# A running maximum spread over the partitions through DRAM instead of by 32-row products: an mLSTM cell and its SwiGLU block

## The chip, the cores and the metric

The kernel runs on one core of one Trainium2 chip. The core has TensorE (products, written PE in the profile, its weight loads PEld), VectorE (DVE), ScalarE (ACT), GpSimd (POOL) and SyncE (SP, which here only issues transfers), and 16 DMA engines that they share. The metric is the device time of one execution in microseconds; less is better. The median of the runs is used.

## The reference, cut to what matters

The first part is an mLSTM cell (batch 4, 8 heads, 768 tokens, heads of 40), given as a loop over tokens:

```python
for t in range(S):
    m_new = np.maximum(f_gate[:, :, t] + m, i_gate[:, :, t])
    f_stab = np.exp(f_gate[:, :, t] + m - m_new)
    i_stab = np.exp(i_gate[:, :, t] - m_new)
    m = m_new
    C = f_stab * C + i_stab * np.einsum('bhd,bhe->bhde', vt, kt)
    n = f_stab * n + i_stab * kt
    h_tilde = np.einsum('bhde,bhe->bhd', C, qt)
    denom = np.maximum(np.abs(np.einsum('bhd,bhd->bh', n, qt)[:, :, None]), 1.0)
    y[:, :, t] = sigmoid(o_gate[:, :, t]) * h_tilde / denom
```

The second part treats y as 3072 tokens of 320 features: out = (silu(x @ w_gate) * (x @ w_val)) @ w_out, with 1536 hidden features. The weights arrive as fp64, everything else as fp32, and all products are in fp32.

## The kernel before, in words

**Tiling.** The 768 tokens of a batch are cut into six chunks of 128 (the constant L). A chunk of a batch is a unit; batch b has units 6b to 6b + 5, 24 in all. Within a chunk the recurrence is written in closed form: F is the running sum of f, g = i - F, and M the running maximum of g and of what is carried in. Token s then acts on token t >= s with the weight w[s, t] = exp(g_s - M_t). The gates lie with a row per (batch, head), so on 32 partitions (f_sb, i_sb, F_sb, g_sb, M_sb, lines 68 to 139). The weights w need g with the token s on the partition (g_T, made by transposes) and M_t the same on all 128 partitions.

**Spreading M.** `weigh(b)` (line 222) makes w for the six chunks of a batch. For each head a product with 32 rows is used: one column of the negated identity `nid`, repeated 128 times, is the stationary operand, and M_sb of the chunk the moving one, so that each of the 128 output rows holds -M of that head (`nm`, line 230; 8 of them in a chunk, 192 in four batches of six chunks, which the profile counts as 384 matrix instructions since an fp32 product takes two here). VectorE adds g (line 232, twice in a chunk), GpSimd sets the part with t < s to -1e30 (line 234), ScalarE takes the exponential (line 236). The w tiles live in a pool of NB + 1 = 7 buffers.

**The cell of a unit** has five stages: `turn` loads the k, q, v and o of the unit two later, weighs v with w's last column (v_w, GpSimd) and transposes k and q; `scores` takes the k.q products (sp) and multiplies them with w on VectorE (s_sb, line 264); `attend` has the products with the state (inter), for the state (add) and with v (intra); `rows` normalises and applies the o gate's sigmoid; `seam` transposes the result into xT. k and q, v, and o have rings of three buffers.

**The block of a batch** has 30 steps: twice twelve `hidden` steps (gv_ps: six products with wg_sb, six with wv_sb; then a sigmoid on ScalarE, line 345, and two multiplications on VectorE, lines 346 and 347) and three `project` steps (o_ps, line 352). The first half of the steps reads the xT of chunks 0 to 2, the second that of 3 to 5. gv_ps and o_ps share two PSUM buffers.

**Order.** The program first weighs batch 0 and runs its cell, with the 24 pieces of the fp64 weights converted among the stages (`weight`, lines 195 to 209, on VectorE, ScalarE and GpSimd). Then, for each batch, the next batch is weighed and its cell's 30 stages run one after each of the block's 30 steps. This program order is a priority only: the Tile framework's planner writes the order of each engine's instructions by simulating the program, and issues on each engine the first in priority whose operands and buffers are ready at that point. At run time each engine then keeps that order and waits where something is late. SP's queue holds the loads of the cells and the stores of the output, ACT's queue those of the weights.

Of the kernel before, what the change touches and what calls it, by code (L numbers as in the profile page):

```python
# [9 lines left out]
F32 = mybir.dt.float32  # L10
U32 = mybir.dt.uint32
AF = mybir.ActivationFunctionType
ALU = mybir.AluOpType
AX = mybir.AxisListType
PSUM = bass.MemoryType.PSUM

L = 128  # tokens of a chunk
NEG = -1e30
# [3 lines left out]
def kernel(  # L22
# [12 lines left out]
):  # L35
    """mLSTM in chunks of 128 tokens, then the SwiGLU block, all in fp32.

    Within a chunk, F is the running sum of f, g = i - F and M the running maximum of g and of the m carried in, so
    that m = F + M. A token s adds exp(g_s - M_t) (k_s.q_t) [v_s, 1] to token t >= s, the state C of the chunks before
    adds exp(m_in - M_t) C q_t. No exponent is above 0 whatever the gates are. Weights that come as fp64 (as the bits  # L40
    of their words) are rounded to fp32 on the way in.
    """
    nc = tc.nc
    B, H, S, D = q.shape
    BH = B * H
    NB = S // L
    PR = H // 2  # pairs of heads, a head in each half of the partitions
    DP = 64
    D1 = D + 1
# [7 lines left out]
    const = ctx.enter_context(tc.tile_pool(name="const", bufs=1))  # L57
    wpool = ctx.enter_context(tc.tile_pool(name="wpool", bufs=1))
    dpool = ctx.enter_context(tc.tile_pool(name="dpool", bufs=NB + 1))
# [3 lines left out]
    psum = ctx.enter_context(tc.tile_pool(name="psum", bufs=2, space=PSUM))  # L63
    gates_scope = ExitStack()
    gates = gates_scope.enter_context(tc.tile_pool(name="gates", bufs=1))

# [1 line left out]
    f_sb = gates.tile([BH, NB, L], F32)  # L68
# [35 lines left out]

# [1 line left out]
    ident = const.tile([128, 128], F32)  # L106
    make_identity(nc, ident)
    idb = ident[0:BH, 0:BH]
    nid = const.tile([BH, BH], F32)
    nc.vector.tensor_scalar(nid, idb, scalar1=-1.0, scalar2=None, op0=ALU.mult)  # L110
    # which pair a row of the gates belongs to, and which half
    pair = const.tile([BH, B * PR], F32)
    nc.vector.reduce_sum(pair, idb.rearrange("p (a two) -> p a two", two=2), axis=AX.X)
    half = const.tile([BH, 2], F32)
    nc.vector.reduce_sum(half, idb.rearrange("p (a two) -> p two a", two=2), axis=AX.X)
    halves = const.tile([BH, 2, DP], F32)
    nc.vector.tensor_copy(halves, half.unsqueeze(2).to_broadcast([BH, 2, DP]))
    # a pair's state is kept whole; a head's own part of it is its half's columns
    own = const.tile([128, 2 * D1], F32)
# [8 lines left out]

# [1 line left out]
    def flat(t):  # L130
        return t.rearrange("p c t -> p (c t)")
# [5 lines left out]
    nc.vector.tensor_copy(step[:, 1:, 0:1], F_sb[:, 0:NB - 1, L - 1:L])  # L137
    M_sb = const.tile([BH, NB, L], F32)
    nc.vector.tensor_tensor_scan(flat(M_sb), flat(step), flat(g_sb), NEG, op0=ALU.add, op1=ALU.max)
    m_in = gates.tile([BH, NB - 1, 1], F32)  # L140
    nc.vector.tensor_add(m_in, M_sb[:, 0:NB - 1, L - 1:L], F_sb[:, 0:NB - 1, L - 1:L])
# [3 lines left out]

    # token on the partition: g_T[t, c, bh] and, for the chunks from the second, e_T
    g_T = const.tile([128, NB, BH], F32)
# [6 lines left out]

    # the decay of a whole chunk, spread over the partitions of the state
    dec_r = gates.tile([BH, NB - 1, B * PR], F32)
# [9 lines left out]

# [1 line left out]
    conv_scope = ExitStack()  # L168
# [4 lines left out]
    def weight(dst, src):  # L173
# [15 lines left out]
        else:  # L189
            nc.scalar.dma_start(out=raw, in_=src.bitcast(U32))  # L190
        words = raw.rearrange("p (n two) -> p n two", two=2)
        lo, hi = words[:, :, 0], words[:, :, 1]
        # The upper word's 20 bits of mantissa with 8 of its 11 bits of exponent; 0 for what fp32 has no exponent for.
        top = tmp("top", U32)
# [5 lines left out]
                                       op0=ALU.is_ge, op1=ALU.mult)  # L200
        # The lower word's bits, scaled by the sign and the power of two, round into it.
        power = tmp("power", U32)
# [15 lines left out]

# [1 line left out]
    w_tiles = {}  # L220

    def weigh(b):
        for c in range(NB):
            w = w_tiles[b * NB + c] = dpool.tile([128, 2, PR, L], F32, name="w_sb", tag="w")
            g2 = g_T[:, c, b * H:(b + 1) * H].rearrange("p (j two) -> p two j", two=2)
            for two in range(2):
                nm = psum.tile([128, PR, L], F32, name="nm", tag="att")
                for j in range(PR):
                    row = b * H + 2 * j + two
                    nc.tensor.matmul(nm[:, j, :], lhsT=nid[:, row:row + 1].to_broadcast([BH, 128]), rhs=M_sb[:, c, :],  # L230
                                     start=True, stop=True)
                nc.vector.tensor_tensor(w[:, two], nm, g2[:, two].unsqueeze(2).to_broadcast([128, PR, L]), op=ALU.add)  # L232
            wf = w.rearrange("p a j t -> p (a j) t")
            nc.gpsimd.affine_select(wf, wf, compare_op=ALU.is_ge, fill=NEG, base=0, pattern=[[0, H], [1, L]],  # L234
                                    channel_multiplier=-1)
            nc.scalar.activation(wf, wf, AF.Exp)

# [1 line left out]
    state = {}  # L239
    xts = {}  # L240

    def turn(u):
        un = units[u]
        load(u + NR - 1)
        un["v_w"] = work.tile([128, H, D1], F32, name="v_w")
        last = w_tiles[u][:, :, :, L - 1].rearrange("p two j -> p j two").unsqueeze(3).to_broadcast([128, PR, 2, D1])
        nc.gpsimd.tensor_tensor(un["v_w"].rearrange("p (j two) d -> p j two d", two=2),  # L247
                                un["v"].rearrange("p (j two) d -> p j two d", two=2), last, op=ALU.mult)
        for n, name in enumerate(("kT", "qT")):
            tp = psum.tile([128, PR, L], F32, name="tp_kq", tag="tr")  # L250
            for j in range(PR):
                nc.tensor.transpose(tp[:, j, :], un["kq"][:, n, 2 * j:2 * j + 2, :].rearrange("p h d -> p (h d)"), ident)  # L252
            un[name] = work.tile([128, PR, L], F32, name=name)
            nc.scalar.copy(un[name], tp)  # L254

    def scores(u):
        un = units[u]
        un["s"] = work.tile([128, 2, PR, L], F32, name="s_sb")
        for two in range(2):
            sp = psum.tile([128, PR, L], F32, name="sp", tag="att")  # L260
            r = slice(two * DP, two * DP + DP)
            for j in range(PR):
                nc.tensor.matmul(sp[:, j, :], lhsT=un["kT"][r, j, :], rhs=un["qT"][r, j, :], start=True, stop=True)  # L263
            nc.vector.tensor_tensor(un["s"][:, two], sp, w_tiles[u][:, two], op=ALU.mult)

# [64 lines left out]

# [1 line left out]
    hs = {}  # L332
# [31 lines left out]

# [1 line left out]
    weigh(0)  # L366
# [10 lines left out]
    for b in range(B):  # L377
        cell = []
# [41 lines left out]
```

## Time and profile before

| what | value |
|---|---|
| runs | 925.11, 924.93 and 929.82 us; median 925.11 |
| the profiled execution: time by its span, first to last instruction | 925.1 us |
| TensorE busy | 875.6 us (95%) |
| VectorE busy | 337.9 us (37%) |
| ScalarE busy | 156.1 us (17%) |
| GpSimd busy | 120.8 us (13%) |
| mean granted TensorE clock | 0.939 |
| moved by DMA | 32.22 MB, 35 GB/s on average |

How to read it: a row such as `L230 PE MATMUL nm<-M_sb,nid ... x384 | 79.9, 395 | 2.1 <-DVE w_sb L232` is a group of instructions: its line, engine, what it writes and reads, how many, their busy time in us and the mean in ns, and the idle time of the engine just before them with what ended it. The chain of waits goes back from the last instruction to what released each. In the chain by time and in timelines, a row starts with the start and the length in us. In rows of stretches come the length, then the busy time of PE, PEld, DVE, ACT and POOL, then the granted TensorE clock (1.00 is full speed), the DMA engines' share and GB/s. A row of DMA issues ends with the KB of one transfer and the median time from issue to landing.

### The profile page before, as it was taken

How to read it: one execution, taken by the hardware profiler on the slowest of the kernel's cores; microseconds unless marked ns; L12 is line 12 of the kernel's file. 1: busy time of each engine (PE TensorE's matmuls, PEld its weight loads, DVE VectorE, ACT ScalarE, POOL GpSimd, SP SyncE). 2: the span in 40 equal slices, each digit the busy share in tenths (PEclk: the TensorE clock that was granted, in tenths of full speed). 3: DMA queues.
4: the chain of work that ended last, by engine and by line, in shares of the span. 5: the costliest groups of instructions: out<-in, count | busy, mean ns of one | idle time of the engine just before them, and what ended most of it. 6: DMA issues, size and time to landing. Idle time of an engine off the chain costs nothing.

```text
span 925.1 us, 8778 instructions
## 1 busy us (share of the span) xinstructions
PE 875.6 (95%) x3477; PEld 553.0 (60%) x3477; DVE 337.9 (37%) x625; ACT 156.1 (17%) x274; POOL 120.8 (13%) x127
## 2 busy tenths in 40 slices
PE   6856769999999999999999999999999999999998
PEld 5755557855665568755665568655755565445445
DVE  5588877433214322334213322234313321210220
ACT  2322122311111112311111112311111101100110
POOL 2344434400000001100000002100000000000000
PEclk9999855599999999799999998799999999999999
DMA  9244454011021111011111110011100000000000
GB/s 139 64 108 112 116 132 114 1 21 30 15 44 21 29 18 33 7 25 27 27 31 22 29 29 22 7 29 22 37 14 1 1 8 14 1 0 22 0 1 21
DMA packets 107273, 32.22 MB, mean 35 GB/s; under 512 B 100640, under 2 KB 103712, under 8 KB 107232
## 3 DMA queue, kind: packets, MB, share of 16 engines
q1 hardware_dynamic: 103392, 19.87, 12.0%
q10 hardware_dynamic: 3840, 11.80, 4.1%
q8 instruction: 27, 0.44, 0.2%
q14 instruction: 14, 0.11, 0.0%
HBM read 27.72 MB, written 3.93 MB: 34 GB/s over the span
## 4 chain that ended last, share of the span: by engine, by line
PE 92%; DVE 3%; issue 1%; DMA 1%; POOL 1%; ACT 0%; ACTq 0%; DVEq 0%; POOLq 0%
PE gv_ps L341 49%; PE o_ps L352 17%; PE nm L230 8%; PE intra L293 5%; PE sp L263 5%; PE inter L273 3%; PE tp_kq L252 3%; PE add L280 2%; PE tp_x L319 1%; DVE top L196 1%; POOL wv_sb L209 0%; DVE size L204 0%; DMA raw<-in_moe_w_gate_dram 0%; DVE top L195 0%; DVE power L203 0%
## 5 line engine op out<-in xcount | busy, mean ns | idle before, releaser
L341 PE MATMUL gv_ps<-xT,wg_sb 128*128 128x384 f32 (+1 forms) x576 | 237.4, 531 | 0.0
L341 PE MATMUL gv_ps<-xT,wv_sb 128*128 128x384 f32 (+1 forms) x576 | 233.5, 526 | 0.0
L341 PEld LDWEIGHTS gv_ps<-xT,wv_sb 128*128 128x128 f32 (+1 forms) x576 | 94.4, 190 | 130.2 <-issue 103.6
L352 PE MATMUL o_ps<-wo_sb,h_sb 128*128 128x320 f32 x576 | 159.3, 435 | 0.0
L341 PEld LDWEIGHTS gv_ps<-xT,wg_sb 128*128 128x128 f32 (+1 forms) x576 | 96.1, 194 | 99.8 <-issue 76.5
L352 PEld LDWEIGHTS o_ps<-wo_sb,h_sb 128*128 128x128 f32 x576 | 108.1, 190 | 44.7 <-issue 1.1
L346 DVE TENSOR_TENSOR sg<-sg,gv_ps 128x384 f32<-128x384 f32 x96 | 53.1, 553 | 221.7 <-ACT sg L345 221.7
L345 ACT ACTIVATE sg<-gv_ps 128x384 f32<-128x384 f32 x96 | 47.1, 490 | 335.7 <-PE gv_ps L341 335.6
L347 DVE TENSOR_TENSOR h_sb<-sg,gv_ps 128x384 f32<-128x384 f32 x96 | 53.2, 554 | 118.8 <-PE gv_ps L341 118.8
L230 PE MATMUL nm<-M_sb,nid 32*128 32x128 f32 x384 | 79.9, 395 | 2.1 <-DVE w_sb L232 1.1
L230 PEld LDWEIGHTS nm<-M_sb,nid 32*128 32x128 f32 x384 | 76.0, 300 | 5.8 <-DVE w_sb L232 3.6
L247 POOL TENSOR_TENSOR v_w<-va,w_sb 128x328 f32<-128x328 f32 x24 | 18.1, 752 | 315.0 <-PE add L280 254.3
L293 PEld LDWEIGHTS intra<-va,s_sb 128*128 128x128 f32 x384 | 54.2, 221 | 3.5 <-issue 0.3
L293 PE MATMUL intra<-va,s_sb 128*128 128x41 f32 x384 | 53.8, 306 | 0.0
L263 PEld LDWEIGHTS sp<-qT,kT 64*128 64x128 f32 x384 | 47.1, 228 | 10.8 <-ACT qT L254 4.8
L263 PE MATMUL sp<-qT,kT 64*128 64x128 f32 x384 | 48.6, 324 | 3.2 <-ACT qT L254 3.2
L232 DVE TENSOR_TENSOR w_sb<-nm,g_T 128x512 f32<-128x512 f32 x48 | 33.2, 691 | 39.6 <-PE nm L230 39.4
L310 POOL TENSOR_TENSOR x_sb<-o_sb,y_sb 128x320 f32<-128x320 f32 x24 | 20.8, 869 | 190.3 <-DVE y_sb L296 187.2
L252 PE MATMUL tp_kq<-ident,kq 128*128 128x128 f32 x192 | 34.1, 323 | 7.3 <-DVE xT L324 5.2
L319 PE MATMUL tp_x<-ident,x_sb 128*128 128x128 f32 (+1 forms) x72 | 14.9, 323 | 25.5 <-DVE x_sb L311 25.5
L252 PEld LDWEIGHTS tp_kq<-ident,kq 128*128 128x128 f32 x192 | 25.5, 164 | 20.6 <-issue 9.9
L234 POOL TENSOR_SCALAR_AFFINE_SELECT w_sb<-w_sb 128x1024 f32<-128x1024 f32 x24 | 26.6, 1108 | 82.5 <-DVE w_sb L232 82.5
(70 smaller groups left out, 494.3 us busy)
## 6 DMA issues: line engine op xcount, KB each, us to landing
kq<-in_k_dram SPq DMA_DIRECT2D x24, 160.0 KB, 3.0
kq<-in_q_dram SPq DMA_DIRECT2D x24, 160.0 KB, 2.8
va<-in_v_dram SPq DMA_DIRECT2D x24, 160.0 KB, 2.6
o_sb<-in_o_gate_dram SPq DMA_DIRECT2D x24, 160.0 KB, 2.6
raw<-in_moe_w_out_dram ACTq DMA_DIRECT2D x6, 640.0 KB, 4.0
out_dram<-z_sb SPq DMA_DIRECT2D x24, 160.0 KB, 1.8
raw<-in_moe_w_gate_dram ACTq DMA_DIRECT2D x6, 512.0 KB, 3.7
raw<-in_moe_w_val_dram ACTq DMA_DIRECT2D x6, 512.0 KB, 3.6
```

The lines of the kernel that those rows point to most:

```text
L230: nc.tensor.matmul(nm[:, j, :], lhsT=nid[:, row:row + 1].to_broadcast([BH, 128]), rhs=M_sb[:, c, :], start=True, stop=True)
L232: nc.vector.tensor_tensor(w[:, two], nm, g2[:, two].unsqueeze(2).to_broadcast([128, PR, L]), op=ALU.add)
L234: nc.gpsimd.affine_select(wf, wf, compare_op=ALU.is_ge, fill=NEG, base=0, pattern=[[0, H], [1, L]], channel_multiplier=-1)
L252: nc.tensor.transpose(tp[:, j, :], un["kq"][:, n, 2 * j:2 * j + 2, :].rearrange("p h d -> p (h d)"), ident)
L263: nc.tensor.matmul(sp[:, j, :], lhsT=un["kT"][r, j, :], rhs=un["qT"][r, j, :], start=True, stop=True)
L273: nc.tensor.matmul(inter[:, 2 * j:2 * j + 2, :].rearrange("p h d -> p (h d)"), lhsT=un["qT"][:, j, :], rhs=state["C"][:, j, :], start=True ...
L293: nc.tensor.matmul(intra[:, h, :], lhsT=un["s"][:, h % 2, h // 2, :], rhs=un["v"][:, h, :], start=True, stop=True)
L341: nc.tensor.matmul(p, lhsT=w_sb[0:dn, kc, ts(m, 128)], rhs=xts[b][0:dn, kc, ts(n, TW)], start=(kc == 0), stop=(kc == NKC - 1))
L345: nc.scalar.activation(sg, ps[0], AF.Sigmoid)
L346: nc.vector.tensor_tensor(sg, sg, ps[0], op=ALU.mult)
L347: nc.vector.tensor_tensor(hs[b, n][:, m, :], sg, ps[1], op=ALU.mult)
L352: nc.tensor.matmul(p, lhsT=hs[b, n][:, m, ts(i, 128)], rhs=wo_sb[:, m, :], start=(m == 0), stop=(m == NFC - 1))
```

## The change

M no longer passes through TensorE. After the scan that makes it, M_sb (32 rows of 768) is stored into a scratch tensor in DRAM, M_dram. For each chunk one transfer then reads the eight heads' 128 values and writes them to all 128 partitions, straight into the w tile: the source has a step of 0 over the partitions, so that each partition receives eight runs of 512 bytes. VectorE computes g - M in one subtraction over 1024 elements from SBUF to SBUF, where it had two additions over 512 elements from PSUM; GpSimd's select and ScalarE's exponential stay as they are. The heads in the w tile now stand in their own order instead of even ones first, and `scores` and `turn` read it by other strides. M_sb moves to the pool of the gates, whose memory the weights' conversion uses later; `nid` is gone.

```diff
-    nid = const.tile([BH, BH], F32)
-    nc.vector.tensor_scalar(nid, idb, scalar1=-1.0, scalar2=None, op0=ALU.mult)
...
-    M_sb = const.tile([BH, NB, L], F32)
+    M_sb = gates.tile([BH, NB, L], F32)
     nc.vector.tensor_tensor_scan(flat(M_sb), flat(step), flat(g_sb), NEG, op0=ALU.add, op1=ALU.max)
+    M_dram = tc.dram_tile([BH, S], F32, name="M_dram")
+    nc.sync.dma_start(out=M_dram, in_=flat(M_sb))
...
         for c in range(NB):
-            w = w_tiles[b * NB + c] = dpool.tile([128, 2, PR, L], F32, name="w_sb", tag="w")
-            g2 = g_T[:, c, b * H:(b + 1) * H].rearrange("p (j two) -> p two j", two=2)
-            for two in range(2):
-                nm = psum.tile([128, PR, L], F32, name="nm", tag="att")
-                for j in range(PR):
-                    row = b * H + 2 * j + two
-                    nc.tensor.matmul(nm[:, j, :], lhsT=nid[:, row:row + 1].to_broadcast([BH, 128]), rhs=M_sb[:, c, :],
-                                     start=True, stop=True)
-                nc.vector.tensor_tensor(w[:, two], nm, g2[:, two].unsqueeze(2).to_broadcast([128, PR, L]), op=ALU.add)
-            wf = w.rearrange("p a j t -> p (a j) t")
-            nc.gpsimd.affine_select(wf, wf, compare_op=ALU.is_ge, fill=NEG, base=0, pattern=[[0, H], [1, L]],
+            w = w_tiles[b * NB + c] = dpool.tile([128, H, L], F32, name="w_sb", tag="w")
+            src = M_dram[b * H:(b + 1) * H, ts(c, L)].unsqueeze(0).to_broadcast([128, H, L])
+            nc.sync.dma_start(out=w, in_=src)
+            gb = g_T[:, c, b * H:(b + 1) * H].unsqueeze(2).to_broadcast([128, H, L])
+            nc.vector.tensor_tensor(w, gb, w, op=ALU.subtract)
+            nc.gpsimd.affine_select(w, w, compare_op=ALU.is_ge, fill=NEG, base=0, pattern=[[0, H], [1, L]],
                                     channel_multiplier=-1)
-            nc.scalar.activation(wf, wf, AF.Exp)
+            nc.scalar.activation(w, w, AF.Exp)
...
-        last = w_tiles[u][:, :, :, L - 1].rearrange("p two j -> p j two").unsqueeze(3).to_broadcast([128, PR, 2, D1])
-        nc.gpsimd.tensor_tensor(un["v_w"].rearrange("p (j two) d -> p j two d", two=2),
-                                un["v"].rearrange("p (j two) d -> p j two d", two=2), last, op=ALU.mult)
+        last = w_tiles[u][:, :, L - 1:L].to_broadcast([128, H, D1])
+        nc.gpsimd.tensor_tensor(un["v_w"], un["v"], last, op=ALU.mult)
...
-            nc.vector.tensor_tensor(un["s"][:, two], sp, w_tiles[u][:, two], op=ALU.mult)
+            w2 = w_tiles[u].rearrange("p (j two) t -> p two j t", two=2)
+            nc.vector.tensor_tensor(un["s"][:, two], sp, w2[:, two], op=ALU.mult)
```

## The prediction

> **What bounds the kernel now.** I read the page's totals and chain first, then the chain in order of time, then stretches of it.
>
> ```profile
> span 925.1 us, 8778 instructions
> PE 875.6 (95%) x3477; PEld 553.0 (60%) x3477; DVE 337.9 (37%) x625; ACT 156.1 (17%) x274; POOL 120.8 (13%) x127
> ...
> PE 92%; DVE 3%; issue 1%; DMA 1%; POOL 1%; ACT 0%; ACTq 0%; DVEq 0%; POOLq 0%
> ...
> L230 PE MATMUL nm<-M_sb,nid 32*128 32x128 f32 x384 | 79.9, 395 | 2.1 <-DVE w_sb L232 1.1
> ...
> L234 POOL TENSOR_SCALAR_AFFINE_SELECT w_sb<-w_sb 128x1024 f32<-128x1024 f32 x24 | 26.6, 1108 | 82.5 <-DVE w_sb L232 82.5
> ```
>
> TensorE is the bound: busy 95% of the span and 92% of the chain. The products that the change removes (nm) are 79.9 us of it. Whether those 79.9 us come back is a question of place, so here is the chain at them, and at undisturbed and following gv products:
>
> ```profile
> 16.55 8.61 PE nm L230 x40
> ...
> 144.32 2.00 PE nm L230 x8
> ...
> 149.46 2.00 PE nm L230 x8
> ...
> 160.50 2.07 PE nm L230 x8
> 162.59 7.19 PE nm L230 x32
> ...
> 171.36 8.83 PE nm L230 x40
> ...
> 268.48 4.46 PE gv_ps L341 x12
> ...
> 361.24 17.34 PE nm L230 x96
> 378.58 6.65 PE gv_ps L341 x12
> ...
> 566.29 17.57 PE nm L230 x96
> 583.86 6.41 PE gv_ps L341 x12
> ```
>
> Four bursts, one per batch: at the start, around 144 to 180, at 361 and at 566. The last two are solid blocks of TensorE time. The first two lie in the stretch where the weights are converted, which the next view (stretches: length, then busy time of PE, its loads, DVE, ACT and POOL, then granted clock, DMA share, GB/s) shows:
>
> ```profile
> 0.00:14.50 14.50, 5.88 (x28) 5.48 (x28) 8.56 (x16) 3.92 (x5) 3.67 (x16) 1.00 1.20 139
> 100.00:120.00 20.00, 13.85 (x64) 11.09 (x64) 17.66 (x31) 4.29 (x9) 8.29 (x7) 0.74 0.43 99
> 142.00:162.00 20.00, 18.20 (x65) 13.99 (x65) 16.48 (x29) 5.92 (x9) 8.24 (x5) 0.50 0.34 92
> 162.00:184.00 22.00, 21.98 (x86) 18.47 (x86) 10.26 (x16) 7.15 (x7) 9.68 (x9) 0.50 0.00 1
> 184.00:200.00 16.00, 16.00 (x64) 9.52 (x64) 6.13 (x12) 1.92 (x4) 2.23 (x3) 0.87 0.18 31
> 361.24:378.58 17.34, 17.34 (x97) 16.95 (x97) 7.89 (x12) 6.98 (x8) 6.88 (x7) 0.63 0.03 10
> ```
>
> Up to about 162 VectorE is the fuller engine (17.66 of 20 us at 100 to 120, 16.48 of 20 at 142); from 162 on it is TensorE (21.98 of 22). In the burst at 361 TensorE is busy without a gap, and still the granted clock averages 0.63: the 32-row products do not hold the clock up. The gv group behind them takes 6.65 us instead of 4.46.
>
> **The change, part by part.** Removed are 384 products with their weight loads; 48 additions become 24 subtractions; 24 loads and one store are added. *Bursts at 361 and 566.* Half of the products lie here: 17.34 + 17.57 = 34.9 us fall away. The next instruction is the first gv group, which needs xT of chunks 0 to 2 only, long copied, so I put nothing in their place. The clock comes back too: (6.65 - 4.46) + (6.41 - 4.46) = 4.1 us. Together **-39.0**.
>
> A rule of the Trainium skill speaks against the second part: "TensorE: Matmul & The Clock Gate", Part 1, says that the clock is released by TensorE being busy and falls back after idle windows, so gapless work should run at full clock. The measurement differs (17.34 of 17.34 us busy, 0.63). By the page alone the clock terms of this sum would be nothing, and it would end some 7 us higher.
>
> *Burst at 144 to 180.* The pieces from 162.59 on, 7.19 + 8.83 = 16.0, stand where TensorE is full: all gained. The 6.1 us before (2.00 + 2.00 + 2.07) stand beside a VectorE at 16.48 of 20, which still has to convert; I take half, 3. Between 0 and 6.1 both ends stay. Clock: at 162 to 184 the other products take 22.0 - 16.0 = 6.0 at 0.50, so 3.0 could come back, and 16 x 0.13 = 2.1 at 184 to 200; less 2.0 for waking, about what a gv group lost behind the later bursts, 3.1. Together **-22.1**.
>
> *The start.* Here a wait is added: M is stored, then read back.
>
> ```profile
> 5.68 1.75 DVE L139 TENSOR_TENSOR_SCAN M_sb<-step,g_sb 32x768 f32<-32x768 f32 x1
> ...
> 11.71 1.19 SPq L96 DMA_DIRECT2D o_sb<-in_o_gate_dram  x1
> ...
> 37.84 0.69 DVE L264 TENSOR_TENSOR s_sb<-sp,w_sb 128x512 f32<-128x512 f32 x1 [1.63 <-PE sp L263]
> ```
>
> ```profile
> kq<-in_k_dram SPq DMA_DIRECT2D x24, 160.0 KB, 3.0
> ...
> raw<-in_moe_w_gate_dram ACTq DMA_DIRECT2D x6, 512.0 KB, 3.7
> ...
> f_sb<-in_f_gate_dram SPq DMA_DIRECT2D x1, 96.0 KB, 2.0
> ```
>
> ```profile
> L136 DVE TENSOR_TENSOR g_sb<-i_sb,F_sb 32x768 f32<-32x768 f32 x1 | 0.9, 937 | 0.0
> L143 DVE TENSOR_TENSOR e_sb<-m_in,M_sb 32x640 f32<-32x640 f32 x1 | 0.8, 811 | 0.0
> L236 ACT ACTIVATE w_sb<-w_sb 128x1024 f32<-128x1024 f32 x24 | 25.3, 1056 | 49.6 <-POOL w_sb L234 47.4 <-issue 2.2
> L345 ACT ACT_TABLE_LOAD x3 | 3.8, 1283 | 0.1
> ```
>
> M is there at 7.43, but SP's queue is issuing the first units' loads until 12.90, and I assume the store queues behind all of them. The store has the size of the f_gate load, 2.0: 14.9. No row shows a broadcast read. One chunk is 512 KB in 1024 runs of 512 bytes. The nearest rows are a 160 KB load in 1024 runs (3.0) and a 512 KB one in long runs (3.7). Bounds 3.0 and 6.7 (both costs added); I take 3.7, as these runs are longer than those of the 160 KB load. The one subtraction per chunk replaces two additions: 0.126 us per 128 elements between L143 and L136 gives 0.937 + 2 x 0.126 = 1.19 us. With the select (1.11) and the exponential (1.06) the first weights are there at 14.9 + 3.7 + 1.19 + 1.11 + 1.06 = 22.0, where VectorE now multiplies with them at 37.84 because unit 0's scores stand behind the nm products in TensorE's order: 15.8 us earlier. Not all of it stays, since VectorE's conversions set the pace later. Bounds 0 and 15.8; I take **-9**, a little over half, because VectorE is free 2 to 4 us in 20 there.
>
> *Moved work.* The chunks of batches 1 to 3 no longer wait for TensorE. The planner issues what is ready when an engine is free:
>
> ```profile
> 400.23 0.80 POOL L310 TENSOR_TENSOR x_sb<-o_sb,y_sb 128x320 f32<-128x320 f32 x1 [0.79 <-DVE y_sb L298]
> ...
> 401.06 0.37 SPq L96 DMA_DIRECT2D o_sb<-in_o_gate_dram  x1
> ...
> 403.77 0.47 ACT L303 ACTIVATE o_sb<-o_sb 128x320 f32<-128x320 f32 x1 [1.42 <-DMA o_sb<-in_o_gate_dram]
> ```
>
> Unit 12 has just read its o; unit 15's is loaded into that buffer at once and passed through the sigmoid three units ahead of its turn. With seven w buffers, the chunk of unit u+7 will likewise be loaded when unit u's scores are done: units 6 to 12 fall into the conversion stretch, units 13 to 23 (11 chunks) among the gv groups. Each of the single exponentials then costs ScalarE up to two table loads, 2 x 1.28 + 1.06 = 3.6 us between sigmoids at least 4.46 apart. What covers it:
>
> ```profile
> 395.08 2.40 PE L341 MATMUL gv_ps<-xT,wv_sb 128*128 128x384 f32 x6
> ...
> 395.71 0.56 DVE L346 TENSOR_TENSOR sg<-sg,gv_ps 128x384 f32<-128x384 f32 x1 [2.11 <-ACT sg L345]
> ```
>
> The gate buffer is free at 396.27, TensorE wants it at 397.48 at the earliest: 1.2 us of slack. Per chunk the stall is therefore between 0 and 3.6 - 1.2 = 2.4 us, 0 to 26 in all. Unit u's attend products follow and widen the gap just where the exponential comes, so I take 0.4 each, **+4**. In the conversion stretch six chunks add 6 x 1.19 = 7.1 us to VectorE and some table loads; bounds 0 (its free time takes them) and 6 x (1.19 + 1.28) = 15; I take **+4**.
>
> "ScalarE: Activation LUTs" of the Trainium skill, What ACT_TABLE_LOAD costs, advises against just this: it counts a drain of 1380 ns beside the 1283 ns load. The row above has the 1283; no row shows the drain apart. By the page's price the 22 loads would hold ScalarE another 30 us, by an estimate up to 893 for the whole.
>
> *SP's queue.* 25 transfers are added there. Queued behind a w load that waits for its buffer are the loads of a unit two or three ahead and output stores; ScalarE's sigmoids wait for the o loads:
>
> ```profile
> ACT o_sb L303 <- DMA o_sb<-in_o_gate_dram: 81.2, 20, 7.7
> ```
>
> It does so now, 20 times and up to 7.7 us, in stretches in which TensorE has no gap. I cost it at nothing; uncovered it would be one w load each, 11 x 3.7 = 41. The buffers' layout in s_sb and v_w changes strides, not sizes: nothing. M_sb's memory passes to the conversions' buffers, which now wait for the store's end (14.9) too; their first load starts later than that anyway, so nothing:
>
> ```profile
> 16.62 0.40 ACTq L190 DMA_DIRECT2D raw<-in_moe_w_gate_dram  x1
> ```
>
> **Sum:** -39.0 - 22.1 - 9 + 4 + 4 = -62.1; 925.1 - 62.1 = **863**. The span of 925.1 equals the runs' median of 925.11, so no offset is added.
>
> **Rivals.**
> *Table switching.* The single exponentials break the sigmoids' rhythm every time. For it: today the six exponentials of a batch stand in one block, with one load back to the sigmoid per batch (three rows of L345 for batches 1 to 3). Against: 1.2 us of slack and ScalarE at 17%. Its price is the upper bound, 26 instead of 4, and 12 instead of 4 before: 863 + 22 + 8 = **893**.
> *Loads at the seam.* The planner keeps the chunks of a batch together at its start. Six subtractions then stand in VectorE's order ahead of the first gv group's. Six loads take 3.7 + 5 x 3.77 (512 KB at the start's 139 GB/s) = 22.6, with the subtraction 23.8; TensorE has one gv group, 4.46, before it runs out of gv buffers: 19 lost of 17.4 saved, twice. If each further load takes only the 1.7 by which the 3.7 row exceeds the 2.0 one, it is 3.7 + 8.5 + 1.2 - 4.5 = 9. So 863 + 2 x (9 to 19) = 881 to 901, say **890**. For it: today's nm blocks stand just there; the o row of unit 15 speaks against.
> *Slow broadcast: slower than before.* 128 partitions read the same 512 bytes, and no row shows what that does. VectorE waits in order for each chunk, and TensorE behind it. With T per load and about 5.7 us covered (3.7 planned, 2 of slack), the loss is 11 (T - 5.7) + (T - 3.7) at the start + half of 6 (T - 5.7) in the conversion stretch. At T = 10 that is 60 + 6 = 67 and the gain is gone: that is the point, 52 GB/s against the 139 at the start. Against it: the slowest of the loads above lands in 3.7. At T = 12 the loss is 96: 863 + 96 = **959**.
> *All of the start stays.* 15.8 instead of 9, nothing for moved work: 863 - 7 - 8 = **848**.
> That the products stay is not possible: their line is gone.
>
> **How the numbers follow.** Forecast 0.58 (its own range 847 to 882, from the start's bounds and 1 to 2 us per chunk), table switching 0.14, loads at the seam 0.11, slow broadcast 0.07, all of the start 0.10. The range 842 to 898 takes in all but the slow broadcast and the tails of the two cases near 890, some 0.15 together. Runs of before lie 0.5% apart, so less than that is no change (920.5 to 929.7). Faster 0.91: all cases but the slow broadcast, less a tail; same 0.03, slower 0.06, both from slow broadcasts with T around and above 10.
>
> **What would show it.** No nm rows; gv groups follow the o_ps products at 361 and 566 at 4.46 us, with clock near 1.00. Unit 0's s_sb near 22. A w load lands in 3 to 7 us. ScalarE has many more table loads, with TensorE gaps of about 0.4 us behind them. It is wrong if VectorE's subtractions wait for DMA while gv groups wait for VectorE, or if the conversion stretch ends later than now.

## The result and the profile after

The kernel after takes 872.67 us (median of 4 runs, 872.53 to 878.03); the kernel before took 927.47 beside it. The ratio is 0.940, with a 95% interval of 0.935 to 0.945. The profiled execution has a span of 870.9 us, 54.2 less than the 925.1 of before; the figures below are set against these two spans. Over all sets of runs the kernel before took between 924.93 and 934.65 us and the kernel after between 872.53 and 878.03, while each span is that of one execution; so a difference of spans of a few us says less than its decimals suggest.

From the page after: the totals, the shares of the chain by engine, and the groups of the changed lines.

```profile
span 870.9 us, 8041 instructions
PE 788.9 (91%) x3093; PEld 473.9 (54%) x3093; DVE 343.2 (39%) x600; ACT 194.0 (22%) x304; POOL 131.2 (15%) x127
...
PE 85%; DVE 6%; issue 3%; POOL 2%; DMA 2%; ACT 1%; ACTq 0%; POOLq 0%; DVEq 0%
...
L230 POOL TENSOR_SCALAR_AFFINE_SELECT w_sb<-w_sb 128x1024 f32<-128x1024 f32 x24 | 33.4, 1397 | 139.3 <-DVE w_sb L229 139.3
...
L229 DVE TENSOR_TENSOR w_sb<-g_T,w_sb 128x1024 f32<-128x1024 f32 x24 | 34.5, 1444 | 12.8 <-DMA w_sb<-M_dram 12.8
...
w_sb<-M_dram SPq DMA_DIRECT2D x24, 512.0 KB, 4.2
```

TensorE is busy for 86.7 us less, more than the 79.9 of the nm products, since the gv groups that followed the bursts at 361 and 566 run faster too. But 54.2 and not 86.7 came off the span: 32.5 us are new idle time of TensorE. Where it lies, the stretch up to 180 shows (length, busy time of PE, PEld, DVE, ACT and POOL, granted clock, DMA share, GB/s), before and after:

```profile
0.00:180.00 180.00, 133.83 (x571) 115.67 (x571) 127.96 (x225) 48.27 (x71) 71.76 (x68) 0.80 0.45 101
```

```profile
0.00:180.00 180.00, 101.53 (x442) 81.05 (x443) 145.56 (x226) 67.79 (x88) 86.41 (x74) 0.81 0.61 145
```

TensorE is idle for 46.2 of these 180 us before and for 78.5 after, 32.3 more: all of it. Behind 180 TensorE's idle time is 3.3 us before and 3.5 after, the same. A second mark divides the span: the first project product (o_ps). It stands behind the first twelve hidden steps, and the first product that these write (h_sb) waits for the last converted piece of the weights, since its tile lies in the memory that the conversion used:

```profile
168.82 1.02 DVE L343 TENSOR_TENSOR h_sb<-sg,gv_ps 128x384 f32<-128x384 f32 x2 [0.79 <-POOL wo_sb L210]
```

Rows of o_ps and of the pieces of wo, with the first and the last start, before and after:

```profile
L352 PE MATMUL o_ps<-wo_sb,h_sb x576: 432/432/537, 244.9 to 921.4; 128*128 128x320 f32 x192
...
L209 POOL TENSOR_TENSOR wo_sb<-top,size x6: 1569/1824/2277, 137.8 to 164.6; 128x640 f32<-128x640 f32 x6
```

```profile
L348 PE MATMUL o_ps<-wo_sb,h_sb x576: 432/432/537, 230.1 to 867.1; 128*128 128x320 f32 x192
...
L210 POOL TENSOR_TENSOR wo_sb<-top,size x6: 1561/1889/2062, 138.2 to 167.2; 128x640 f32<-128x640 f32 x6
```

Up to the first o_ps the change gains 14.8 us, from there to the last one 39.5. And the conversion of the weights ends 2.6 us *later* than before.

### The profile page after: what moved, and what is told of

Read it like the earlier page. It is cut to its first block, busy times and chain, and to the rows that moved or that the text cites. A ratio compares the mean times of both kernels' runs of the same rounds, so it can differ in the third digit from the quotient of the medians.

```text
span 870.9 us, 8041 instructions
## 1 busy us (share of the span) xinstructions
PE 788.9 (91%) x3093; PEld 473.9 (54%) x3093; DVE 343.2 (39%) x600; ACT 194.0 (22%) x304; POOL 131.2 (15%) x127
## 4 chain that ended last, share of the span: by engine, by line
PE 85%; DVE 6%; issue 3%; POOL 2%; DMA 2%; ACT 1%; ACTq 0%; POOLq 0%; DVEq 0%
PE gv_ps L337 50%; PE o_ps L348 18%; PE intra L289 5%; PE sp L258 4%; PE inter L269 2%; PE tp_kq L247 2%; PE add L276 2%; DMA raw<-in_moe_w_gate_dram 2%; DVE top L200 1%; DVE top L196 1%; PE tp_x L315 1%; DVE top L197 1%; DVE power L204 1%; DVE size L205 1%; POOL w_sb L230 1%
## 5 line engine op out<-in xcount | busy, mean ns | idle before, releaser
L337 PE MATMUL gv_ps<-xT,wg_sb 128*128 128x384 f32 (+1 forms) x576 | 232.0, 522 | 0.1
L243 POOL TENSOR_TENSOR v_w<-va,w_sb 128x328 f32<-128x328 f32 x24 | 21.0, 876 | 277.5 <-PE add L276 229.1
L230 POOL TENSOR_SCALAR_AFFINE_SELECT w_sb<-w_sb 128x1024 f32<-128x1024 f32 x24 | 33.4, 1397 | 139.3 <-DVE w_sb L229 139.3
L258 PEld LDWEIGHTS sp<-qT,kT 64*128 64x128 f32 x384 | 44.8, 217 | 13.4 <-ACT qT L249 8.3
L258 PE MATMUL sp<-qT,kT 64*128 64x128 f32 x384 | 46.8, 313 | 5.9 <-ACT qT L249 5.9
L232 ACT ACTIVATE w_sb<-w_sb 128x1024 f32<-128x1024 f32 x24 | 25.2, 1055 | 70.6 <-POOL w_sb L230 70.6
L306 POOL TENSOR_TENSOR x_sb<-o_sb,y_sb 128x320 f32<-128x320 f32 x24 | 22.8, 952 | 111.4 <-DVE y_sb L292 107.7
L229 DVE TENSOR_TENSOR w_sb<-g_T,w_sb 128x1024 f32<-128x1024 f32 x24 | 34.5, 1444 | 12.8 <-DMA w_sb<-M_dram 12.8
L247 PEld LDWEIGHTS tp_kq<-ident,kq 128*128 128x128 f32 x192 | 26.0, 165 | 22.8 <-DVE xT L320 10.3
L320 DVE COPY xT<-tp_x 64x128 f32<-64x128 f32 x24 | 6.7, 281 | 77.6 <-ACT xT L317 77.6
```

Of the source, the lines that this page charges most:

```text
L229: nc.vector.tensor_tensor(w, gb, w, op=ALU.subtract)
L230: nc.gpsimd.affine_select(w, w, compare_op=ALU.is_ge, fill=NEG, base=0, pattern=[[0, H], [1, L]], channel_multiplier=-1)
L232: nc.scalar.activation(w, w, AF.Exp)
L337: nc.tensor.matmul(p, lhsT=w_sb[0:dn, kc, ts(m, 128)], rhs=xts[b][0:dn, kc, ts(n, TW)], start=(kc == 0), stop=(kc == NKC - 1))
```

## The experiments

Each was run beside the kernel before; where none is given a ratio, it is a single execution. "The end of the conversion" is the start of the last wo piece in the row of that kernel.

**One activation table.** The sigmoids are computed as (1 + tanh(x/2))/2, so that ScalarE no longer changes its table between exponential and sigmoid.

```diff
-        nc.scalar.activation(sg, ps[0], AF.Sigmoid)
-        nc.vector.tensor_tensor(sg, sg, ps[0], op=ALU.mult)
+        nc.scalar.activation(sg, ps[0], AF.Tanh, scale=0.5)
+        nc.vector.scalar_tensor_tensor(sg, in0=sg, scalar=1.0, in1=ps[0], op0=ALU.add, op1=ALU.mult)
...
-        nc.scalar.copy(z, p)
+        nc.scalar.mul(z, p, 0.5)
```

(The o gate likewise; its two multiplications change places between VectorE and GpSimd.)

> The changed kernel with every sigmoid(x) written as (1 + tanh(x/2))/2, so that exponentials and gates share one table set: one table load instead of 39. Same result, same DMA, same products. Theory A (the stretch of the weight conversion is paced by the hand-overs between VectorE and GpSimd, 24 pieces of about 6 us): 869 to 874, the last piece still ends near 168. Theory B (the 16 table loads in that stretch, 1.28 us each, hold up the conversion's squares and the copies of kT, qT and xT): 858 to 867, the last piece ends before 163. From 200 us on nothing changes by either theory, since TensorE has no gaps there now.

Measured: 864.96 us, ratio 0.930 (0.925 to 0.935), span 863.2. The same two rows in this kernel:

```profile
L348 PE MATMUL o_ps<-wo_sb,h_sb x576: 432/432/537, 222.4 to 859.4; 128*128 128x320 f32 x192
...
L210 POOL TENSOR_TENSOR wo_sb<-top,size x6: 1531/1996/2111, 130.7 to 160.7; 128x640 f32<-128x640 f32 x6
```

The conversion ends 6.5 us earlier, the first o_ps stands 7.7 earlier, and from there on both kernels take the same 637.0. So theory B, and a first answer: with one table the kernel after gains nothing in the dense part and 7 to 8 us in the conversion stretch.

**The same in the kernel before**, as a control.

> The kernel before with the sigmoids as (1 + tanh(x/2))/2, the control for the run with one table. The kernel before has 5 table loads up to 200 us where the kernel after has 19. Theory A (the 7.7 us that the one table gained in the kernel after are the table loads that the change brought into the conversion stretch): here it gains under 3 us, ratio 0.997 or more. Theory B (the gain has to do with the other order of the o gate's multiplications on VectorE and GpSimd, and not with the change): 6 to 10 us here too, ratio 0.989 to 0.994.

Measured: ratio 1.009 (1.005 to 1.012), span 930.3. The whole gains nothing here, theory A: the first o_ps stands at 243.7, 1.2 us earlier, and what lies behind it takes 6.4 us longer than before, for a reason that was not looked for. But the last wo piece starts at 160.5, 4.1 us earlier than before. The kernel after has 19 table loads up to 200 us, where before has 5 and either tanh version 1. Set against the control, the loads that the change brought are worth 7.7 - 1.2 = 6.5 us by the first o_ps and 6.5 - 4.1 = 2.4 us by the end of the conversion; these runs do not settle it closer.

**The chunks of batch 1 late.** Their w loads wait for the last converted piece.

```diff
+            if b == 1:
+                nc.vector.tensor_copy(w[0:1, 0, 0:1], wo_sb[0:1, NFC - 1, DM - 1:DM])
             nc.sync.dma_start(out=w, in_=src)
```

> The changed kernel, but the six chunks of batch 1 are loaded, subtracted, masked and exponentiated only after the last converted weight piece (a one-element copy from it into the w tile stands ahead of the load). Theory A: the stretch gets rid of 6 subtractions of about 1.5 us and 6 selects of 1.5 us, so the last piece ends at 158 to 163 instead of 168.8, and the whole is 862 to 868 unless the six chunks in a row hold up TensorE behind it. Rival (the moved chunks are free, the stretch has its pace from the units' chain): the last piece ends at 167 to 169 and the whole is 872 to 885, since the chunks now come late.

Measured: 869.74 us, ratio 0.936 (0.931 to 0.941), span 867.8. The last wo piece starts at 156.5 instead of 167.2, but the first o_ps comes only at 227.0, 3.1 us earlier: the six chunks, with their loads, subtractions, selects and exponentials, then stand between the conversion and the first hidden steps. Their work moves the end of the conversion by 10.7 us, as theory A has it, but putting it off costs most of that again, and the time lies between the ranges of the two.

**Batch 0 by products**, the others by the transfer.

```diff
+            if b == 0:
+                # 32-row products and additions as in the kernel before
+            else:
                 nc.sync.dma_start(out=w, in_=src)
                 nc.vector.tensor_tensor(w, gb, w, op=ALU.subtract)
```

> The changed kernel, but batch 0's weights get M by the 32-row products as before; batches 1 to 3 by the transfer. Theory A (the conversion sets the pace from 23 us on, so what the transfer gains at the start, 26.8 instead of 37.8 for the first product with w, is lost again): 870 to 876. The prediction's step (9 of the 15.8 us gained at the start stay): 879 to 885.

Measured: 878.19 us, ratio 0.944 (0.938 to 0.950), span 877.5: the transfer is worth 6.6 us at the start by the spans (5.5 by the medians), between what the two theories gave. The first s_sb stands at 37.9 as before, the last wo piece at 174.2.

**Batch 1 by products**, the others by the transfer; the same edit with `b == 1`.

> The kernel after with the M of batch 1 alone spread by the 32-row products again; batches 0, 2 and 3 by the transfer. It prices the burst at 144 to 180 together with the chunks moved into the conversion stretch. Theory A (the prediction's steps, 22.1 gained there and 4 paid for the moved chunks): 18 us slower than the kernel after, 886 to 893. Theory B (what is left of the first part when the start is taken as 6.6 from the run with products in batch 0: 14.8 - 6.6 = 8.2): 876 to 883.

Measured: 882.98 us, ratio 0.949 (0.945 to 0.954), span 880.1. The transfer is worth 9.2 us for batch 1 by the spans (10.3 by the medians), theory B, at the upper end of its range. Its pieces of wo and its nm products in the chain, which again stand behind one another from 152 on as before:

```profile
L212 POOL TENSOR_TENSOR wo_sb<-top,size x6: 1543/1811/2247, 129.4 to 156.2; 128x640 f32<-128x640 f32 x6
```

```profile
152.08 2.07 PE nm L237 x8
154.15 7.19 PE nm L237 x32
161.34 1.58 PE gv_ps L350 x2
162.92 8.83 PE nm L237 x40
```

This run joins the pieces. Its s_sb begins at 30.5, 7.3 us before the 37.8 of the kernel before, its conversion ends 8.4 us before, and its first o_ps, at 239.3, stands 5.6 us before: most of the lead of the start is kept. Giving batch 1 to the transfer too then moves that end by 11.0 us (156.2 to 167.2). If that delay counts in full at the first o_ps, which no run shows by itself, the products that fall away are worth 9.2 + 11.0 = 20.2.

**Each partition its own bytes.** The w loads read bytes of their own for each partition (from q) instead of the same ones for all; the weights are then not M's, and the loads need not wait for the store. The edit changes one thing more: each partition's 4 KB lie in one piece in q, where M has eight runs of 512 bytes. The packets show it, in the kernel after and in this one:

```profile
DMA packets 132278, 44.85 MB, mean 52 GB/s; under 512 B 101040, under 2 KB 128688, under 8 KB 132240
```

```profile
DMA packets 110774, 44.85 MB, mean 52 GB/s; under 512 B 101040, under 2 KB 104112, under 8 KB 110736
```

For the same bytes the packets under 2 KB are 24,576 fewer, which are 24 loads of 1024.

```diff
-            src = M_dram[b * H:(b + 1) * H, ts(c, L)].unsqueeze(0).to_broadcast([128, H, L])
+            src = q.rearrange("b h s d -> (b h s d)")[...].rearrange("(p h t) -> p h t", p=128, h=H)
```

> The changed kernel with each w load reading 1024 different runs of 512 bytes (of q) instead of eight runs repeated for 128 partitions; the output isn't the reference's, as w is made from q. It measures the broadcast read by itself. If repeated reads of the same bytes cost something, a w load lands in 3.0 to 3.7 us here against 4.2; if not, in 4.0 to 4.4, and the whole time stays within 2 us.

Measured: one execution, 867.44 us, span 865.6, 5.3 below the kernel after and so outside the 2 us that were expected. The loads land in 3.4 us (median) instead of 4.2, as expected if repeated addresses cost something. But the 0.8 us are what repeated addresses and shorter pieces cost together; the run does not part them, nor from the 5.3 the share of the earlier first load (8.5 instead of 13.6).

**The kernel before with products of 128 rows**, 96 of them zero.

```diff
-    nid = const.tile([BH, BH], F32)
+    nid = const.tile([128, BH], F32)
+    nc.gpsimd.memset(nid, 0.0)
...
-                    nc.tensor.matmul(nm[:, j, :], lhsT=nid[:, row:row + 1].to_broadcast([BH, 128]), rhs=M_sb[:, c, :],
+                    nc.tensor.matmul(nm[:, j, :], lhsT=nid[:, row:row + 1].to_broadcast([128, 128]), rhs=M_all[:, c, :],
```

> The kernel before, with its nm products over 128 rows of which 96 hold zeros (same values, same count of products). Theory A (the prediction's reading, that 32-row products do not hold the clock up): in the bursts at about 361 and 566 the granted clock goes from 0.63 to 0.95 or more, the gv group behind them takes about 4.5 us instead of 6.65 and 6.41, the burst 17.3 becomes 12 to 17, and the span falls by 4 to 16 us, to 909 to 921. Theory B (it is products of 128 columns with a weight load each that do it, whatever the rows): clock 0.6 to 0.7 in the bursts, gv group behind them above 6, span 923 to 927.

Measured: one execution, 890.25 us, span 888.5, 36.6 less than before. Theory A, and more than it asked for. The chain at the second burst and that stretch:

```profile
340.67 11.49 PE nm L233 x96
352.16 4.46 PE gv_ps L344 x12
```

```profile
340.67:352.16 11.49, 11.49 (x97) 11.09 (x97) 7.89 (x12) 5.94 (x8) 6.87 (x7) 1.00 0.05 16
```

The same 96 matrix instructions take 11.49 us instead of 17.34 at a clock of 1.00 instead of 0.63, and the gv group behind them 4.46 instead of 6.65. With the second such burst (11.49 for 17.57, 4.46 for 6.41 behind it) this is 5.85 + 2.19 + 6.08 + 1.95 = 16.1 of the 36.6; the other 20.5 lie before the first o_ps (224.4), where the first s_sb stands at 29.1 instead of 37.8 and the last wo piece starts at 154.9, 9.7 us earlier. In the first burst too a product takes 275 ns (median up to 40 us) where those of 32 rows take 416.

This kernel also sets a mark for the change. Up to the first o_ps the padded products are 5.7 us *ahead* of the kernel after (224.4 against 230.1); only behind it, where the two remaining bursts stand, the transfer is 23.3 us better (637.0 against 660.3). Padded products for the first two batches and the transfer for the others were not tried.

**The conversion cut short, before and after.** The lower words of the fp64 weights are left out, so that the weights lose their last bits; VectorE's steps power and size fall away, and GpSimd copies instead of adding (for the 24 pieces of the kernel before, 19.0 us instead of 41.3).

```diff
-        power = tmp("power", U32)
-        nc.vector.tensor_scalar(power, top, scalar1=0xFF800000, scalar2=None, op0=ALU.bitwise_and)
-        nc.vector.scalar_tensor_tensor(size, in0=lo, scalar=2.0 ** -52, in1=power.bitcast(F32),
-                                       op0=ALU.mult, op1=ALU.mult)
...
-        nc.gpsimd.tensor_tensor(dst, tf, sz, op=ALU.add)
+        nc.gpsimd.tensor_copy(dst, tf)
```

> The kernel before with the lower words of the fp64 weights left out: lines 203 and 204 (power, size) are gone, which are 11.4 + 17.4 = 28.8 us of VectorE up to 185, and GpSimd copies instead of adding. The weights lose their last bits. Theory A (in the kernel before, TensorE with its nm products is full from 142 on, VectorE only up to there): gains 8 to 20 us, 905 to 918. Theory B (the loads of the weights set the pace in the conversion stretch): gains under 6, 920 or more.

> The kernel after with the same two steps left out (power and size, 14.5 + 17.7 = 32.2 us of VectorE up to 185). Theory A (the missing 12 us of the prediction were lost because VectorE, 16.7 to 19.0 busy of 20 from 20 to 120, is the bound of the conversion stretch): the last piece of wo is there 18 to 32 us earlier than at 168.8, the time is 842 to 856, and the difference to the short kernel before grows from 54 to 60 or more. Theory B (table loads, the w loads or ScalarE's order hold the stretch up): last piece under 12 us earlier, time 860 or more, difference about 54.

Measured: before 905.44 us (ratio 0.974, 0.970 to 0.978), span 898.0, 27.1 less; after 848.21 (ratio 0.912, 0.909 to 0.915), span 845.5, 25.4 less. The kernel after met theory A's time and its last piece (139.0, 28 us earlier), but the difference between the two did not grow to the 60 that it asked for: it is 52.5 us between the spans and 57.2 between the medians. In the kernel before the time of 905.44 lies just inside theory A's range, but the gain, 25.1 by the medians and 27.1 by the spans, is more than its 20. So the conversion, on VectorE and GpSimd, sets the pace up to the dense part in *both* kernels; it is not something that the change brought about. Which of the two engines it is these runs do not part, since the edit relieves both.

**One table, and no subtraction.** ScalarE takes exp(-M + g) with g as its bias, in eight pieces of 128 columns.

```diff
-            nc.vector.tensor_tensor(w, gb, w, op=ALU.subtract)
...
-            nc.scalar.activation(w, w, AF.Exp)
+            for h in range(H):
+                nc.scalar.activation(w[:, h, :], w[:, h, :], AF.Exp, scale=-1.0, bias=g_T[:, c, b * H + h:b * H + h + 1])
```

> The kernel after with the sigmoids as (1 + tanh(x/2))/2 as in the run with one table, and without VectorE's subtraction: ScalarE takes the exponential of -M + g itself, with g as its bias, in 8 pieces of 128 columns per chunk (8 x 0.26 = 2.1 us instead of 1.06, from 0.49 for 384 and 1.06 for 1024 columns); GpSimd's select writes +1e30 ahead of it. 13 or 14 chunks up to 160 take some 1.6 us each from VectorE, 21 us. Theory A (VectorE bounds the conversion stretch): last piece of wo 10 to 20 us before the 162.2 of the run with one table, time 847 to 857. Theory B (once the table loads are gone, GpSimd and the loads set the pace): last piece within 5 us of 162, time 860 to 867.

Measured: 867.27 us, ratio 0.932 (0.928 to 0.936), span 864.5. Theory A falls, and the time is 0.3 us above theory B's range: from 20 to 160 VectorE is busy for 106.4 us instead of the 133.3 of the run with one table, and the last wo piece still starts at 162.5 (160.7 there). VectorE now waits instead, longest for intra products (9.2 and 5.4 us up to 170):

```profile
DVE y_sb L291 <- PE intra L288: 9.2, 4, 5.0
DVE xT L319 <- ACT xT L316: 6.9, 4, 2.7
```

The work taken from one engine in order was put on another one in the same loop of hand-overs. So it seems from these waits; no run shows it by itself, and how much of the subtraction's time can be had back at all stays open.

**Hidden steps in the idle time.** Since TensorE is idle for 78.5 us up to 180, the first twelve hidden steps of batch 0 are written among the last stages of its cell, and their h tile gets memory of its own instead of the conversions'. With one table.

```diff
+    hpool = [ctx.enter_context(tc.tile_pool(name="hpool0", bufs=1))]
     conv_scope = ExitStack()
...
+        if NB // 2 * 5 <= n < NB // 2 * 5 + NFC:
+            hidden(0, 0, n - NB // 2 * 5)
     conv_scope.close()
-    hpool = ctx.enter_context(tc.tile_pool(name="hpool", bufs=2))
+    hpool.append(ctx.enter_context(tc.tile_pool(name="hpool1", bufs=1)))
```

> The kernel after with one table (as e1_tanh, 865) and with the first twelve hidden steps of batch 0 written among the last stages of batch 0's cell, one per stage from unit 3 on; their h tile has its own memory, so that they need not wait for the conversions' buffers, and the second half's h tile takes the conversions' memory afterwards. Theory A (TensorE's idle time up to the end of the conversion, 78 us in the kernel after, some 32 of it from 80 to 160, is what is left over of the start's lead, and these steps can use it): 10 to 25 us faster than with one table alone, 840 to 856. Theory B (VectorE, which takes 1.1 us more per step, 13 in all, pushes the conversion's end back by as much as TensorE gains): 860 to 870.

Measured: 828.62 us, ratio 0.891 (0.887 to 0.895), span 825.8, the fastest version here, its span 37.4 us below that of the run with one table: theory A, by more than it allowed. The stretch from 80 to 160, in the kernel after and in this one:

```profile
80.00:160.00 80.00, 47.53 (x221) 38.71 (x221) 70.69 (x114) 30.25 (x42) 39.83 (x28) 0.67 0.56 144
```

```profile
80.00:160.00 80.00, 72.00 (x282) 39.73 (x283) 71.81 (x123) 23.65 (x40) 33.32 (x24) 0.98 0.45 122
```

The conversion ends later than in the run with one table (168.8, not 160.7), as theory B feared, but TensorE has done 24 us more in that stretch, and at a clock of 0.98 instead of 0.67. Room for an h tile of its own (12 x 384 fp32 numbers, 18 KB per partition) may in part come from the change: M_sb's 3 KB no longer lie among the constants. Whether the kernel before has the room, and what these early steps would gain there, was not tried; their gain is not one of the change.

## Why the prediction was right, and where it was not

The sum was -62.1, measured were -54.2. The mechanism was right: the bound engine gave its time back in full where it had no gap. The miss of 7.9 is smaller than that of the worst step, 8.9, because another step missed by 4 the other way. The steps in turn:

**Bursts at 361 and 566, -39.0: right.** In the chain of the kernel after the batches now begin at 346.24, 531.55 and 717.07, the last with twelve gv groups in a row:

```profile
346.24 4.46 PE gv_ps L337 x12
...
531.55 4.46 PE gv_ps L337 x12
...
717.07 55.64 PE gv_ps L337 x144
```

A batch takes 185.3 and 185.5 us instead of the 205.05 from 361.24 to 566.29: 39.3 for the two. That the 32-row products held the clock down, the run with 128 rows shows. The 0.63 is a mean: up to 366.24 the clock of the burst at 361 is 0.94, from there to its end 0.50. The rule of the Trainium skill ("TensorE: Matmul & The Clock Gate", Part 1) that a busy array runs at full clock holds for the 128-row products (1.00) and not for the 32-row ones (0.63), both without a gap.

**Eleven chunks among the gv groups, +4: nothing was lost.** Every single exponential does bring its table loads, 39 in all where before had 9. But none of it reaches TensorE; by the sum's reasoning the slack of 1.2 us and the attend products hide it. The whole stretch of a batch has no gap, and with one table the dense part takes the same 637.0:

```profile
346.24:531.55 185.31, 185.31 (x771) 110.39 (x771) 61.18 (x115) 43.53 (x70) 18.34 (x21) 1.00 0.19 41
```

```profile
364.91 2.38 PE L337 MATMUL gv_ps<-xT,wg_sb 128*128 128x384 f32 x6
...
365.69 1.06 ACT L232 ACTIVATE w_sb<-w_sb 128x1024 f32<-128x1024 f32 x1 [3.91 <-POOL w_sb L230]
...
366.76 1.28 ACT L341 ACT_TABLE_LOAD   x1
...
368.06 0.49 ACT L341 ACTIVATE sg<-gv_ps 128x384 f32<-128x384 f32 x1
```

The gate's group ends at 367.29, its sigmoid starts at 368.06, 0.8 us late, and TensorE does not stop. The rival of table switching falls here. So does the price that the Trainium skill gives in "ScalarE: Activation LUTs", What ACT_TABLE_LOAD costs, a drain of 1380 ns beside each load: the load starts 0.01 us after the exponential's end, and the sigmoid 0.02 us after the load's.

**The start, -9: a little too much, since the lead was smaller.** It was worth 6.6 us. The first s_sb stands at 26.8, 11.0 earlier, not 15.8. The timeline, and the piece of the chain that goes with it:

```profile
9.85 0.98 SPq L140 DMA_DIRECT2D M_dram<-M_sb  x1
...
17.82 1.23 DVE L229 TENSOR_TENSOR w_sb<-g_T,w_sb 128x1024 f32<-128x1024 f32 x1 [1.46 <-DMA w_sb<-M_dram]
19.18 1.09 POOL L230 TENSOR_SCALAR_AFFINE_SELECT w_sb<-w_sb 128x1024 f32<-128x1024 f32 x1 [15.94 <-DVE w_sb L229]
22.79 0.67 ACT L199 ACTIVATE size<-raw 128x512 f32<-128x512 f32 x1 [4.19 <-DMA raw<-in_moe_w_gate_dram]
23.37 1.04 ACT L232 ACTIVATE w_sb<-w_sb 128x1024 f32<-128x1024 f32 x1
```

```profile
16.16 6.61 DMA raw<-in_moe_w_gate_dram
```

M came back sooner than assumed, since its store was issued at 9.85, ahead of the last loads. But the first exponential, ready at 20.3, stands in ScalarE's order behind a square of the conversion, which waited until 22.79 for its raw weights. These took 6.6 us to land, where such a load took 3.7 before; the w loads issued from 13.60 on run on the same DMA engines, which is the likely cause but was not tried apart. The estimate that a little over half of the lead stays was near: 6.6 of 11.1 in the run with products in batch 0, and 5.6 of 7.3 at the first o_ps in the run with products in batch 1.

**The burst at 144 to 180, -22.1, and six chunks in the conversion stretch, +4: the step that failed.** Predicted were 18.1 together, measured 9.2. The step reads "In the conversion stretch six chunks add 6 x 1.19 = 7.1 us to VectorE and some table loads; ... I take +4", and its size was wrong: the chunks moved there put the end of the conversion back by 11.0 us (run with batch 1 by products), 10.7 (run with batch 1 late). The bounds of 0 to 15 held it; the value taken within them did not. Of the 11, 2.4 to 6.5 us are table loads by the runs with one table, which the sum had named and then mostly given away to VectorE's free time. The rival of table switching had 12 here, so this half of it came close. Of the miss of 8.9, 7.0 are the chunks, and 1.9 are left to the burst itself (20.2, by the reckoning above, for 22.1). The prediction also named a sign of its being wrong that came true here: the conversion stretch ends later than before, by 2.6 us. The single subtractions were too cheap, too. In the stretch up to 168 and behind 190 they read:

```profile
L229 DVE TENSOR_TENSOR w_sb<-g_T,w_sb x12: 1208/1628/2309, 24.0 to 163.8; 128x1024 f32<-128x1024 f32 x12
```

```profile
L229 DVE TENSOR_TENSOR w_sb<-g_T,w_sb x10: 1218/1220/1226, 206.0 to 484.8; 128x1024 f32<-128x1024 f32 x10
```

Behind 190 they take 1.22 (1.19 was predicted), up to 168, where GpSimd is busier, 1.63. The additions of before, with one operand in PSUM, did not stretch there:

```profile
L232 DVE TENSOR_TENSOR w_sb<-nm,g_T x12: 676/692/692, 20.1 to 164.7; 128x512 f32<-128x512 f32 x12
```

This fits a rule of the Trainium skill: "SBUF — State Buffer", Who interferes with whom, has a VectorE instruction with both inputs in SBUF share its second read port with GpSimd's reads. The select stretches as well, to 1574 ns up to 168 (13 of them) against 1197 behind 190. That the port is the cause was not tried apart from the rest.

**The rivals.** The slow broadcast fell: 4.2 us median landing, near the 3.7 taken, and 0.8 above loads of 4 KB pieces without repeated bytes. Loads at the seam fell: no batch begins with a wait. Nothing was lost on SP's queue in the dense part: the stretch above has no gap. That all of the start stays fell too, with 6.6 us of its 15.8.

**The steps together.** -39.3, -6.6, -9.2 and 0 make -55.1, near the -54.2 measured. Against the prediction the burst at 144 with its six chunks missed by +8.9, the start by +2.4, and the chunks among the gv groups by -4.0. That these partly cancel is luck.

## What to carry to other kernels

Taking work off the bound engine gives its full time only where that engine has no gap; the same edit gained all of its 39 us in the dense stretch but 9.2 of some 20 us in the stretch where another engine had to keep up, because what replaced it (a VectorE pass, a longer select, table loads) landed on the engines that set the pace there. Price a moved step by the end that it shifts, not by the mean free time of the engine that takes it. And before a product is replaced because it is slow, look at the granted clock in its row, and at how long its products take: with 96 rows of zeros beside its 32, the kernel before gains 36.6 us, where the transfer gains 54.2.

## What the runs showed of the hardware that was not expected

- Gapless fp32 products of 32 rows ran at a mean granted clock of 0.63 (0.94 in the first 5 us, then 0.50), those of 128 rows with three quarters zeros at 1.00.
- The clock that a row gives for the beginning of a trace need not be the one that the products had. From 40 to 60 us the kernel with 128 rows has 0.50 in its row and the kernel before 1.00:

```profile
40.00:60.00 20.00, 12.37 (x59) 11.16 (x58) 15.97 (x29) 4.12 (x8) 8.43 (x7) 0.50 0.43 106
```

```profile
40.00:60.00 20.00, 12.00 (x57) 10.80 (x56) 16.67 (x28) 6.25 (x10) 8.85 (x7) 1.00 0.44 112
```

But an sp product takes 438 ns on average in both, and 278 from 200 to 300 us in both, and the 32-row products up to 40 us take 416 ns (median) at a recorded 1.00, as in the burst at 361, most of which has 0.50. So the durations do not bear out the early 1.00; why it is recorded stays open.
- Table loads of 1283 ns: the 20 behind 200 us cost nothing, where ScalarE has 1.2 us of slack per group; the 19 up to there cost some us, where it feeds a chain of hand-overs.
- A VectorE subtraction from SBUF to SBUF took between 1.21 and 2.31 us, longest in the stretch where GpSimd was busiest.
